# Pooled attention and a gated FFN on one core: three small tiles are resized so that TensorE's FFN operands start at one rest by 256 bytes

## The chip, the core and the metric

The kernel runs on one core of one Trainium2 chip. The metric is the device time of one execution in microseconds (us). Before the change it is 1043.09 us, the median of 3 runs (1041.45 to 1043.99). Lower is better.

## What is computed

Attention over keys and values that are averaged in groups of 8 along the sequence, followed by an FFN with a SiLU gate on the root-mean-square-normed result. All data is fp32; the shapes are B = H = 8, S = 576, D = 64, 4608 tokens, d_model 512, d_ff 1536.

```python
def _attn_ref(q, k, v):
    B, H, S, D = q.shape
    pool = 8
    Sp = S // pool
    k_p = k.reshape(B, H, Sp, pool, D).mean(axis=3)
    v_p = v.reshape(B, H, Sp, pool, D).mean(axis=3)
    scores = (1.0 / np.sqrt(D)) * np.matmul(q, k_p.transpose(0, 1, 3, 2))
    scores = scores - np.max(scores, axis=-1, keepdims=True)
    attn = np.exp(scores)
    attn = attn / (np.sum(attn, axis=-1, keepdims=True) + 1e-09)
    return np.matmul(attn, v_p)

def _moe_ref(x, w_gate, w_val, w_out, rms_g):
    rms = np.sqrt(np.mean(x * x, axis=-1, keepdims=True) + 1e-06)
    xn = x / rms * rms_g
    g = xn @ w_gate
    silu = g * (1.0 / (1.0 + np.exp(-g)))
    return silu * (xn @ w_val) @ w_out
```

## The kernel before

**Numbers.** TensorE takes fp32r operands (a rounded fp32 form). To keep precision, each FFN operand is split into a high part (rounded) and a low part (what the rounding left); a product is then three matmuls: high by high, low by high, high by low.

**Tiling.** The tokens are cut into 9 blocks of NB = 512, d_ff into NF = 12 slices of 128, d_model into NC = 4 chunks of 128. Every FFN matmul has a stationary operand of 128x128, which a LDWEIGHTS puts into the array, and a moving operand of 128x512. There are 3744 of them, of four sorts:

- `mm1` (line 812): x times w_gate or w_val, into a PSUM tile `psg`. Stationary: the weight slices `w1_f`. Moving: the high and low parts `xh`, `xl` of the block's tokens. 12 matmuls per (block, slice, gate or value).
- `mm2` (line 853): the activations times w_out, into four PSUM tiles `po`. Stationary: the activations' low part `hl` and high part `hh`, in four pieces of 128 tokens. Moving: the weight rows `w2_f`. Where nothing stands against it the four `hl` matmuls come first, then eight `hh` matmuls: for each of the four pieces one with the weights' high part and one with their low part. 12 matmuls per (block, slice).
- `product` (line 764): in the second part of the run, pairs of token blocks (5 with 6, 7 with 8) are multiplied by the w_gate/w_val slices in seven products in place of eight (Strassen's scheme), into `px` and `py`. Stationary: sums and blocks of weights `wp`, read back from DRAM into a ring of eight SBUF tiles, the ones that held `xh` and `xl`. Moving: sums of token blocks `xp`, in the space of the weights `w1`. 6 matmuls per product.

The attention is computed in the same program between these: scores `pss` (line 390), transposes `pst`, output `psx` (line 471), sums of squares `psr`. Softmax, splits and activations run on ScalarE (ACT), VectorE (DVE) and GpSimd (POOL).

**Order.** Two strings of steps written out by hand, ORDER and LATER, set the order of every engine's instructions; a step is a name and indices (`mg38` is mm1, gate, block 3, slice 8). Nothing is rescheduled.

**Places in SBUF.** Tiles come from pools that lie one behind the other in each partition's memory: `const` (small constants and `prob`), `wp` (the weights, and in the second part `xp`), `sb1` (one buffer a name: `mxe*`, `xh*`, `xl*`, `acc`, `act`, `hl`), `sb2` (two buffers a name: `st`, `xraw`, `out`, `pk`, `pv`, `ptf`, `hh` and small ones). A tile starts where the tile ahead of it ends, rounded up to 32 bytes. So the size of a small tile shifts every tile behind it. Three sizes count here: the unused constant `rest` (line 208, 104 floats, 416 bytes), the four `mxe` tiles of row maxima and sums (line 353, 2x2x5 floats, 80 bytes each, in steps of 96), and the two `pk` tiles of pooled keys (line 336, 72 floats, 288 bytes each).

This document calls the start of an operand modulo 256 bytes its **rest**. The pieces that a matmul reads within an FFN tile start at multiples of 512 bytes in it, so all operands of one tile have the tile's rest. Before the change the FFN tiles have three rests: 0 (`w1`, `w2`, `xp`), 128 (`xh`, `xl`, the ring `wp`, `hl`) and 192 (`hh`).

Of the kernel before, what the change touches and what calls it, by code (L numbers as in the profile page):

```python
# [9 lines left out]
F32 = mybir.dt.float32  # L10
# [7 lines left out]
P = 128  # L18
B, H, S, D = 8, 8, 576, 64
POOL = 8  # L20
SP = S // POOL
# [171 lines left out]
def body(ctx: ExitStack, tc: tile.TileContext, qT, kT, vN, w1, w2, gain, out):  # L193
    nc = tc.nc

    const = ctx.enter_context(tc.tile_pool(name="const", bufs=1))
    wp = ctx.enter_context(tc.tile_pool(name="wp", bufs=1))
    sb1 = ctx.enter_context(tc.tile_pool(name="sb1", bufs=1))
    sb2 = ctx.enter_context(tc.tile_pool(name="sb2", bufs=2))
# [5 lines left out]
    one = const.tile([P, 1], F32, name="one")  # L205
    nc.vector.memset(one, 1.0)
    ones = const.tile([P, 1], F32R, name="ones")
    const.tile([P, 104], F32, name="rest")
    nc.scalar.copy(ones, one)
    gcol = const.tile([P, NC], F32, name="gcol")  # L210
    eps = const.tile([P, 1], F32, name="eps")
# [86 lines left out]
    def own(p):  # L298
        s = st.setdefault((0, p), {})
        if "own" not in s:  # L300
            s["own"] = space1(NF - 2 - 2 * p, [P, 3 * S + SP + P], F32, f"own{p}")
        return s["own"]
# [28 lines left out]
    def s_kpool(b, p):  # L331
        s = st[b, p]
        if b == 0:
            pk = own(p)[:, 3 * S:3 * S + SP]
        else:
            pk = sb2.tile([P, SP], F32, tag="pk", name=f"pk{b}_{p}")
        s["pk"] = pk
        nc.vector.tensor_reduce(pk, s["k"].rearrange("p (s o) -> p s o", o=POOL), AX.X, ALU.add)

# [9 lines left out]
    def s_max(b, p, h):  # L349

        s, n = st[b, p], len(OFFS2)
        if "mx" not in s:
            x = sb1.tile([P, 2, 2, n], F32, tag=f"mxe{p}", name=f"mx{b}_{p}")
            s["mx"], s["sm"] = x[:, 0], x[:, 1]
        mx = s["mx"][:, h, :]
        nc.vector.tensor_reduce(mx, s["ps", h][:, :n * SP].rearrange("p (t k) -> p t k", k=SP), AX.X, ALU.max)
        nc.vector.tensor_scalar(mx, mx, -EXP_SCALE, None, ALU.mult)
# [521 lines left out]
    def first_phase():  # L879
        V, S_, G = nc.vector, nc.scalar, nc.gpsimd  # L880
        steps = dict(
            k=load_k, q=load_q, v=load_v, K=s_kpool, V=s_vpool, S=s_heads, M=s_max, E=s_exp, R=s_inverse,
            N=lambda b, p, h: s_norm(b, p, h, G), T=s_pt,
            C=lambda b, p, h: s_ptcopy(b, p, h, V.tensor_copy), D=lambda b, p, h: s_ptcopy(b, p, h, S_.copy),
            A=s_av, Y=lambda b, p, u: s_xcopy(b, p, u, S_.copy), X=lambda b, p, u: s_xcopy(b, p, u, V.tensor_copy),
            Z=s_xsq, Q=s_square, J=s_join, P=s_tokens, p=s_total, r=s_root, s=s_unroot, B=s_spread, H=s_scale,
            I=first_x, x=first_hi, y=lambda c: first_lo(c, V),
            l=w_load, a=w_abs, b=w_shift, c=w_low, d=w_sign, h=w_hi, w=lambda n: w_lo(n, V), W=lambda n: w_lo(n, G),
            g=lambda f: mm1(0, f, 0), e=lambda f: mm1(0, f, 1), G=lambda f: gate(0, f), F=lambda f: val(0, f),
            i=lambda f: act_hi(0, f), j=lambda f: act_lo(0, f, V), L=lambda f: act_lo(0, f, G), o=lambda f: mm2(0, f),  # L890
            z=warm, t=lambda c: (x_hi(1, c), x_lo(1, c)))
        nc.sync.dma_start(gcol, gain)
        run(ORDER, 1, steps)
        for t in range(NB // P):
            o_copy(0, t)
            o_store(0, t)

    def later_phase():
        V, S_ = nc.vector, nc.scalar
        run(LATER, 2, dict(  # L900
            lk=load_k, lq=load_q, lv=load_v, pk=s_kpool, pv=s_vpool, sc=s_heads, mx=l_max, sb=l_sub, ex=l_exp,
            sm=l_sum, nm=l_norm, tr=l_turn, dm=l_place, av=s_av, xc=l_xcopy, xd=l_xlast, sq=s_square, jn=s_join,
            sh=l_sumhi, sl=l_sumlo, rm=l_total, rt=l_root, rc=l_unroot, rs=l_scale,
            kt=keep_tail, xh=x_hi, xl=x_lo, mg=lambda i, f: mm1(i, f, 0), me=lambda i, f: mm1(i, f, 1), gt=gate,
            vl=val, hi=act_hi, lo=lambda i, f: act_lo(i, f, V), mo=mm2, mp=mm2, ev=o_copy, st=o_store,
            wd=w_blocks, wt=w_whole, wf=w_sum, wh=w_sumhi, wl=w_sumlo, ws=w_store,
            ys=p_sum, yh=p_hi, yl=p_lo, rl=w_part, pr=product,
            cp=lambda i, f: S_.copy(later(i, f), st["X"]),
            u2=lambda i, f: V.tensor_add(u2(i), later(i, f), st["Y"]),
            sa=lambda i, f: S_.activation(new_act(i, f), st["X"], AF.Silu),  # L910
            u3=lambda i, f: V.tensor_add(u3(i), u2(i), st["Y"]),  # L911
            c2=lambda i, f: V.tensor_sub(later(i, f), u3(i), st["X"]),  # L912
            sw=lambda i, f: S_.activation(later(i, f), later(i, f), AF.Silu),  # L913
            v2=lambda i, f: V.tensor_add(u3(i), u3(i), st["Y"]),  # L914
            v1=lambda i, f: V.tensor_add(u2(i), u2(i), st["Y"]),
            va=lambda i, f: V.tensor_mul(st["act"], st["act"], u2(i)),
            vb=lambda i, f: V.tensor_mul(later(i, f), later(i, f), u3(i))))
# [40 lines left out]
```

## Time and profile before

| what | value |
|---|---|
| median of 3 runs | 1043.09 us (1041.45 to 1043.99) |
| the profiled execution: its own time | 1040.0 us |
| its span, first to last instruction | 1037.9 us |
| TensorE clock granted over the span | 0.976 |
| TensorE matmul (PE) busy | 1007.0 us, 97% of the span |
| TensorE weight load (PEld) busy | 790.9 us, 76% |
| VectorE (DVE) busy | 632.0 us, 61% |
| ScalarE (ACT) busy | 449.3 us, 43% |
| GpSimd (POOL) busy | 227.4 us, 22% |
| mean DMA rate | 130 GB/s |

Rows of the profile name the line, the engine, the operation, the tile written and the tiles read (numbers in names left out), the shape, and how often. In rows of the timeline, the first number is the start in us from the start of the span, the second how long the group lasted; instructions of one sort that follow each other are one row. A matmul's own time (some 395 ns for the 128x512 ones) is its latency in a pipeline: the next one starts long before it ends. So the time that a matmul costs is not this duration but the distance from its start to the next one's, which is worked out from two rows that follow each other.

### The profile page before, as it was taken

What the parts mean: (1) busy time and instruction counts of PE and PEld (TensorE: products, weight loads), DVE (VectorE), ACT (ScalarE), POOL (GpSimd) and SP (SyncE); (2) the same over time, 40 slices, a digit from 0 to 9 for tenths busy, and PEclk for the clock granted to TensorE, in tenths of its full rate; (3) what the DMA queues carried; (4) which work ended last, traced back from release to release, by engine and by line L of the source; (5) the groups of instructions that cost most, each with busy time, mean ns of one, the idle gap of its engine ahead of it and who ended that gap; (6) DMA issues with size and microseconds to landing.
All of it is one profiled execution on the core that took longest, in us unless ns stands there. A gap on an engine that the chain in (4) does not pass through costs nothing.

```text
span 1037.9 us, 13861 instructions
## 1 busy us (share of the span) xinstructions
PE 1007.0 (97%) x4850; PEld 790.9 (76%) x4850; DVE 632.0 (61%) x1024; ACT 449.3 (43%) x845; POOL 227.4 (22%) x216
## 2 busy tenths in 40 slices
PE   7999999999999999999999999999999999999987
PEld 6777777777777777777777787878786778888866
DVE  6699996554772964775485385644655764444432
ACT  5767665543473454554364362322333432111121
POOL 2314440144333541355324140000000000000000
PEclk7599999999999999999999999999999999999999
DMA  9345422245345353444244323564544134544311
GB/s 303 126 158 187 171 73 77 71 139 143 102 134 156 100 159 91 140 145 150 83 146 147 97 89 115 162 206 143 167 143 134 41 122 146 151 149 144 102 40 41
DMA packets 97077, 134.71 MB, mean 130 GB/s; under 512 B 10225, under 2 KB 60145, under 8 KB 95729
## 3 DMA queue, kind: packets, MB, share of 16 engines
q1 hardware_dynamic: 97008, 133.83, 41.3%
q8 instruction: 39, 0.64, 0.2%
q14 instruction: 30, 0.24, 0.1%
HBM read 91.23 MB, written 34.60 MB: 121 GB/s over the span
## 4 chain that ended last, share of the span: by engine, by line
PE 86%; DVE 7%; ACT 2%; issue 2%; DMA 1%; SPq 0%; ACTq 0%; DVEq 0%
PE psg L812 28%; PE po L853 26%; PE py L764 13%; PE px L764 10%; PE pss L390 4%; PE psx L471 3%; DVE wt L258 1%; PE pst L447 1%; DVE wt L262 1%; DMA main<-kT 1%; PE psr L555 1%; DVE wt L254 1%; DVE w L280 0%; ACT prob L368 0%; PE psb L579 0%
## 5 line engine op out<-in xcount | busy, mean ns | idle before, releaser
L812 PE MATMUL psg<-xh,w 128*128 128x512 f32 x960 | 304.4, 399 | 1.8 <-ACT act L819 1.8
L853 PE MATMUL po<-w,hh 128*128 128x512 f32 x864 | 227.4, 395 | 0.0
L812 PEld LDWEIGHTS psg<-xh,w 128*128 128x128 f32 x960 | 177.4, 188 | 50.7 <-issue 5.3
L853 PEld LDWEIGHTS po<-w,hh 128*128 128x128 f32 x864 | 163.9, 190 | 36.8
L812 PE MATMUL psg<-xl,w 128*128 128x512 f32 x480 | 189.3, 395 | 0.2 <-DVE xl L642 0.2
L764 PE MATMUL py<-xp,wp 128*128 128x512 f32 x576 | 149.7, 395 | 0.8 <-DVE u L914 0.8
L853 PE MATMUL po<-w,hl 128*128 128x512 f32 x432 | 126.9, 403 | 9.8 <-DVE hl L839 5.1
L764 PEld LDWEIGHTS py<-xp,wp 128*128 128x128 f32 x576 | 108.3, 188 | 27.2 <-DVE u L914 1.2
L764 PE MATMUL px<-xp,wp 128*128 128x512 f32 x432 | 112.7, 396 | 0.0
L812 PEld LDWEIGHTS psg<-xl,w 128*128 128x128 f32 x480 | 90.2, 188 | 21.9 <-DVE xl L642 0.6
L853 PEld LDWEIGHTS po<-w,hl 128*128 128x128 f32 x432 | 79.8, 189 | 34.0 <-DVE hl L839 6.5
L421 POOL TENSOR_TENSOR prob<-prob,sm 128x360 f32<-128x360 f32 x48 | 43.7, 911 | 282.4 <-DVE sm L417 279.9
L764 PEld LDWEIGHTS px<-xp,wp 128*128 128x128 f32 x432 | 81.0, 188 | 20.0 <-ACT xraw L479 0.5
L824 DVE TENSOR_TENSOR act<-act,psg 128x512 f32<-128x512 f32 x60 | 40.8, 681 | 81.7 <-PE psg L812 70.1
L834 ACT CAST hh<-act 128x512 fp32r<-128x512 f32 x84 | 52.1, 621 | 66.0 <-DVE act L824 57.2
L839 DVE TENSOR_TENSOR hl<-act,hh 128x512 fp32r<-128x512 f32 x78 | 58.3, 748 | 34.3 <-ACT hh L834 26.7
L819 ACT ACTIVATE act<-psg 128x512 f32<-128x512 f32 x60 | 35.8, 597 | 67.7 <-PE psg L812 64.1
L819 ACT ACT_TABLE_LOAD x34 | 43.6, 1283 | 38.0 <-DVE hl L839 19.9
L911 DVE TENSOR_TENSOR u<-u,py 128x512 f32<-128x512 f32 x24 | 16.5, 688 | 67.4 <-PE py L764 67.4
L516 POOL TENSOR_TENSOR acc<-acc,sq 128x576 f32<-128x576 f32 x21 | 31.5, 1499 | 102.4 <-ACT sq L510 102.4
L913 ACT ACTIVATE hb<-hb 128x512 f32<-128x512 f32 x24 | 15.2, 632 | 87.8 <-DVE hb L912 87.8
L686 POOL TENSOR_TENSOR wt<-wsum,wt 128x256 fp32r<-128x256 f32 x48 | 38.3, 814 | 53.1 <-ACT wt L682 53.0
(132 smaller groups left out, 1225.0 us busy)
## 6 DMA issues: line engine op xcount, KB each, us to landing
wp<-sum SPq DMA_DIRECT2D x96, 256.0 KB
wp<-blocks SPq DMA_DIRECT2D x72, 256.0 KB
blocks<-w SPq DMA_DIRECT2D x24, 512.0 KB
sum<-wt SPq DMA_DIRECT2D x48, 256.0 KB
wx<-w SPq DMA_DIRECT2D x10, 1024.0 KB
v<-vN SPq DMA_DIRECT2D x32, 288.0 KB
out<-o SPq DMA_DIRECT2D x36, 256.0 KB
wx<-w SPq DMA_DIRECT2D x16, 512.0 KB
```

Source lines behind the costliest of these rows:

```text
L390: nc.tensor.matmul(s["ps", h][:, t * SP:(t + 1) * SP], s["q"][r, o:o + P], s["pk"][r, :], start=True, stop=True)
L421: nc.gpsimd.tensor_tensor(l_pr(h), l_pr(h), sm[:, :, None].broadcast_to([P, len(OFFS2), SP]), ALU.mult)
L471: nc.tensor.matmul(ps[r, :n], s["pv"][:, r], x, start=True, stop=True)
L516: nc.gpsimd.tensor_add(acc[b], acc[b], st[b, p]["sq"])
L686: nc.gpsimd.tensor_sub(y[:, 1], place(f, f"T{k}"), y[:, 0].bitcast(F32))
L764: nc.tensor.matmul(ps[:, :NB], w[:, a, c, :], x[:, b, c, :], start=j == 0 and not more, stop=j == len(todo) - 1, skip_group_check=more)
L812: nc.tensor.matmul(ps[:, :NB], w[:, c, cols], x[c], start=(j == 0), stop=(j == len(todo) - 1))
L819: nc.scalar.activation(t, ps[:, :NB], AF.Silu)
L824: nc.vector.tensor_mul(t, t, ps[:, :NB])
L834: nc.scalar.copy(a, act_in(i, f))
L839: eng.tensor_sub(l, act_in(i, f), hh[i, f].bitcast(F32))
L853: nc.tensor.matmul(po[i][t], x[i, f][:, t * P:(t + 1) * P], w, start=(f == 0 and k == 0), stop=(f == NF - 1 and k == 2))
```

## The change

Nothing is added to or removed from what the engines do. On every engine the built program has the same instructions in the same order, with the same waits on the same values; only the addresses of operands in SBUF differ.

```diff
     ones = const.tile([P, 1], F32R, name="ones")
-    const.tile([P, 104], F32, name="rest")
     nc.scalar.copy(ones, one)
...
         else:
-            pk = sb2.tile([P, SP], F32, tag="pk", name=f"pk{b}_{p}")
+            pk = sb2.tile([P, 96], F32, tag="pk", name=f"pk{b}_{p}")[:, :SP]
         s["pk"] = pk
...
         if "mx" not in s:
-            x = sb1.tile([P, 2, 2, n], F32, tag=f"mxe{p}", name=f"mx{b}_{p}")
-            s["mx"], s["sm"] = x[:, 0], x[:, 1]
+            x = sb1.tile([P, 2, 2, 8], F32, tag=f"mxe{p}", name=f"mx{b}_{p}")
+            s["mx"], s["sm"] = x[:, 0, :, :n], x[:, 1, :, :n]
```

`rest` goes (416 bytes less ahead of `wp`), each `mxe` tile grows from 80 to 128 bytes (four of them, 128 bytes more ahead of `xh`), each `pk` tile from 288 to 384 bytes (two, 192 bytes more ahead of `hh`). The instructions still use 72 and 5 floats of the grown tiles. The places in the built program, as byte starts and rests by 256:

| tile | role in FFN matmuls | before: start, rest | after: start, rest |
|---|---|---|---|
| `prob` (attention) | none | 2208, 160 | 1792, 0 |
| first `w1` tile (all `w1`, `w2`, `xp` alike) | stationary in mm1, moving in mm2 and product | 6144, 0 | 5728, 96 |
| first `xh` (all `xh`, `xl`, ring `wp` alike) | moving in mm1, stationary in product | 160384, 128 | 160096, 96 |
| `act` and `hl` | stationary in mm2 (low part) | 179072 and 181120, 128 | 178784 and 180832, 96 |
| `st`, `xraw`, `out` | none | 128 | 96 |
| the two `pk` (attention) | none | 128 and 160 | 96 and 224 |
| the two `hh` | stationary in mm2 (high part) | 224704 and 226752, 192 | 224608 and 226656, 96 |

So the distance from the moving operand's rest to the stationary operand's rest, by 256, goes from 128 (mm1, product, `hl`) and 192 (`hh`) to 0 throughout.

## The prediction, made before the changed kernel had run

> **What bounds the kernel.** I read the page's busy table first, then the chain of work that ended last.
>
> ```profile
> PE 1007.0 (97%) x4850; PEld 790.9 (76%) x4850; DVE 632.0 (61%) x1024; ACT 449.3 (43%) x845; POOL 227.4 (22%) x216
> ...
> PE 86%; DVE 7%; ACT 2%; issue 2%; DMA 1%; SPq 0%; ACTq 0%; DVEq 0%
> PE psg L812 28%; PE po L853 26%; PE py L764 13%; PE px L764 10%; PE pss L390 4%; PE psx L471 3%; DVE wt L258 1%; PE pst L447 1%; DVE wt L262 1%; DMA main<-kT 1%; PE psr L555 1%; DVE wt L254 1%; DVE w L280 0%; ACT prob L368 0%; PE psb L579 0%
> ```
>
> The busy 97% alone proves nothing, since matmul durations overlap. The chain does: the FFN matmuls (psg, po, py, px) carry 28 + 26 + 13 + 10 = 77% of the 1037.9 us span, about 799 us. The groups of instructions say how many there are and that they wait little:
>
> ```profile
> L812 PE MATMUL psg<-xh,w 128*128 128x512 f32 x960 | 304.4, 399 | 1.8 <-ACT act L819 1.8
> L853 PE MATMUL po<-w,hh 128*128 128x512 f32 x864 | 227.4, 395 | 0.0
> L812 PE MATMUL psg<-xl,w 128*128 128x512 f32 x480 | 189.3, 395 | 0.2 <-DVE xl L642 0.2
> L764 PE MATMUL py<-xp,wp 128*128 128x512 f32 x576 | 149.7, 395 | 0.8 <-DVE u L914 0.8
> L853 PE MATMUL po<-w,hl 128*128 128x512 f32 x432 | 126.9, 403 | 9.8 <-DVE hl L839 5.1
> L764 PE MATMUL px<-xp,wp 128*128 128x512 f32 x432 | 112.7, 396 | 0.0
> ```
>
> That is 960 + 480 + 576 + 432 = 2448 in mm1 and product, 432 with `hl`, 864 with `hh`: 3744. What one costs is its cadence, start to next start, in stretches where nothing waits. First from the chain, then from the timeline of PE alone:
>
> ```profile
> 630.62 5.59 PE psg L812 x24
> ```
> ```profile
> 869.84 0.62 PE L853 MATMUL po<-w,hh 128*128 128x512 f32 x2
> 870.30 1.56 PE L764 MATMUL py<-xp,wp 128*128 128x512 f32 x6
> 871.70 1.56 PE L764 MATMUL px<-xp,wp 128*128 128x512 f32 x6
> ```
> ```profile
> 811.03 1.08 PE L853 MATMUL po<-w,hl 128*128 128x512 f32 x4
> 811.95 2.00 PE L853 MATMUL po<-w,hh 128*128 128x512 f32 x8
> 813.79 1.09 PE L853 MATMUL po<-w,hl 128*128 128x512 f32 x4
> 814.72 1.99 PE L853 MATMUL po<-w,hh 128*128 128x512 f32 x8
> 816.55 1.08 PE L853 MATMUL po<-w,hl 128*128 128x512 f32 x4
> ...
> 838.60 0.40 PE L853 MATMUL po<-w,hl 128*128 128x512 f32 x1
> ```
>
> The reader is to see three cadences. mm1: 5.59 / 24 = 0.2329 us. Product: 871.70 - 870.30 = 1.40 for 6, 0.2333 us. mm2: from 811.03 to 838.60 are 120 matmuls in 27.57 us, 0.2298 us; inside it, four `hl` take 0.92 to 0.93 (0.231 each), eight `hh` 1.84 to 1.83 (0.229 each). The three have the same shapes and the same clock, and mm1 and `hl`, for instance, move their operands in quite different patterns. What sets the `hh` apart is the rest of their stationary operand: 192 against a moving operand at 0, where all others stand 128 apart. **So the trace gives a reason to think that the rests matter, by some 3.6 ns in 233.** A second confound, that an `hh` piece is loaded twice running, is weaker: the interval into the first `hh` piece of a tile is as short as the second.
>
> **Why the cadence can depend on rests at all.** In the weight loads' timeline
>
> ```profile
> 630.92 0.42 PEld L812 LDWEIGHTS psg<-xh,w 128*128 128x128 f32 x2
> 631.38 0.19 PEld L812 LDWEIGHTS psg<-xl,w 128*128 128x128 f32 x1
> ```
> ```profile
> 630.91 0.40 PE L812 MATMUL psg<-xl,w 128*128 128x512 f32 x1
> 631.15 0.63 PE L812 MATMUL psg<-xh,w 128*128 128x512 f32 x2
> ```
>
> the load for the next matmul starts within 0.01 us of the running matmul's start (630.92 after 630.91), lasts 0.19 us, and the next matmul starts some 0.04 us after its end. Both read SBUF at the same time: the moving operand of matmul n and the stationary operand of matmul n+1. The pair whose rests count is that one.
>
> **The change, part by part.** Orders, waits and counts of instructions are unchanged, so no wait appears or goes. Three effects are left.
>
> 1. *The pair's distance becomes 0.* Distance 0 occurs before only at handovers: while the last `hh` matmul of mm2 runs (`w2`, rest 0), the first `w1` piece (rest 0) of the following mm1 is loaded. There are 44 such handovers without a wait; the first and the last:
>
> ```profile
> 68.91 0.40 PE L853 MATMUL po<-w,hh 128*128 128x512 f32 x1
> 69.15 0.40 PE L812 MATMUL psg<-xh,w 128*128 128x512 f32 x1
> ...
> 630.23 0.39 PE L853 MATMUL po<-w,hh 128*128 128x512 f32 x1
> 630.46 0.40 PE L812 MATMUL psg<-xh,w 128*128 128x512 f32 x1
> ```
>
> Their mean interval, from start times that the trace holds to the ns, is 0.2306 us. The control is 95 handovers from an `hh` matmul to an operand at rest 128 (`hl` or the ring), again first and last:
>
> ```profile
> 171.56 0.40 PE L853 MATMUL po<-w,hh 128*128 128x512 f32 x1
> 171.80 0.40 PE L853 MATMUL po<-w,hl 128*128 128x512 f32 x1
> ...
> 1030.97 0.40 PE L853 MATMUL po<-w,hh 128*128 128x512 f32 x1
> 1031.21 0.40 PE L853 MATMUL po<-w,hl 128*128 128x512 f32 x1
> ```
>
> Their mean is 0.2336 us. So from the same preceding work a load at distance 0 comes 3 ns sooner than one at 128, and about 1 ns later than one at 192. I take 0.2306 us as the cadence of the whole FFN after the change. Sum: 2448 x (0.2331 - 0.2306) = 6.1 us gained, 432 x (0.2310 - 0.2306) = 0.2 gained, 864 x (0.2306 - 0.2294) = 1.0 lost; 5.3 us net. Only what lies on the chain counts: 3744 matmuls at a mean of 0.232 are 869 us, of which the chain holds 799, a share of 0.92. That leaves **4.9 us**. Bounds of this unknown: below, all go at the `hh` rate of 0.2294, which gains (2448 x 0.0037 + 432 x 0.0016) x 0.92 = 9.0 us; above, all go at 0.2331, which loses (864 x 0.0037 + 432 x 0.0021) x 0.92 = 3.8 us. I stay at the row of distance 0 itself.
>
> A rule of the skill speaks against any effect here. The Trainium skill, "TensorE: Matmul & The Clock Gate", section "Step-by-step: what each phase is for", says that TensorE has two independent SBUF read ports, so that loading the next tile's weights takes no read bandwidth from the running matmul. By that rule the sum would be 0. The 0.229 of `hh` against 0.233 elsewhere disagrees with it in this trace, or has a cause that I don't see.
>
> 2. *Rest 96 is no multiple of 64.* All FFN operands were at multiples of 64. The nearest rows are scores whose moving operand `pk` lies at 128 and at 160:
>
> ```profile
> 174.68 1.34 PE L390 MATMUL pss<-pk,q 64*128 64x72 f32 x20
> 194.89 1.34 PE L390 MATMUL pss<-pk,q 64*128 64x72 f32 x20
> ```
>
> The first is at 128, the second at 160; both take 1.34 us. They are short and of full fp32, so they don't settle it for 128x512, but I put this at 0, with the bounds from the same two rows: their rounding of 0.01 in 20 matmuls is 0.5 ns on each, or 3744 x 0.0005 x 0.92 = 1.7 us either way.
>
> 3. *ACT, DVE, POOL and DMA see shifted tiles too.* DVE is on the chain with 7%, ACT 2%, DMA 1%. I put them at 0; a 1% change of all three would be 0.01 x 10% x 1038 = 1.0 us either way. The DMA queue's cover is wide in the product phase:
>
> ```profile
> 680.00:780.00 100.00, 77.60 (x320) 60.05 (x321) 1.00 0.53 162
> ```
>
> There (the window's columns are length, PE and PEld busy, clock, DMA share, GB/s) the DMA engines are busy 0.53 of the time, so that transfers could take half as long again before the ring starves TensorE. If that cover were gone, py and px, 23% of the chain, would grow with the transfers.
>
> **The sum.** The profiled execution took 1040.0 us, 2.1 more than its span of 1037.9, and lies 3.1 us below the median shown. 1040.0 - 4.9 = 1035.1 for such an execution; against the median of 1043.09 that is 1038.2 us, 0.47% less. A measurement of this kernel can tell about 0.3% (3.1 us) from no change.
>
> **The rivals.**
>
> - *Distance counts by 128, not by 256* (ends slower). 192 is then 64, the only good distance, and 0 and 128 are the same bad one. mm1 and product don't move, and mm2 loses its better rate: 3.8 us, 1046.9 us. It decides as soon as steady matmuls at distance 0 go at over 0.2320 us, where gains and losses cancel: (2448 x 0.2331 + 432 x 0.2310 + 864 x 0.2294) / 3744 = 0.2320. For it: the good 192 and the bad 128 fit a period of 128 as well. Against it: the 44 handovers at 0.2306. They are single intervals, and the matmul before may have left the pair in a good phase. Chance 0.13.
> - *Rests do nothing* (the change doesn't do what it says, or the gain ends in waits). `hh` is faster for another reason, such as its order of PSUM tiles, and keeps its rate: 1043.1 us. For it: the skill's rule above; against it the control handovers, which start new pieces in new PSUM tiles as the others do. Chance 0.22.
> - *Same rest is as good as 192 or better.* All at 0.2294: 9.0 us less, 1034.1 us. For it: nothing yet shows a steady run at 0. Chance 0.17, of which a part is for still shorter cadences.
> - *Lockstep collides* (slower). Both reads start in the same place at every matmul, and each interval is like the slowest single ones above, 0.24 us: (2448 x 0.0069 + 432 x 0.009 + 864 x 0.0106) x 0.92 = 27.5 us, 1070 us; or rest 96 costs each matmul a part of that. Against it: the shorter handovers at equal rests. Chance 0.07.
>
> **How the numbers follow.** My forecast has 0.41. Around it the cadence may be off by 1 ns, 3.4 us, so a quarter of it ends within 0.3%. Faster by over 0.3% (below 1040.0): three quarters of 0.41, nearly all of 0.17, a little from the second rival, 0.50. Slower by over 0.3% (above 1046.2): 0.07 and the larger half of 0.13, 0.15. Within: 0.35. The range goes from 1033, just under the all-at-`hh` case, to 1047, which takes in the period-128 case; what is left out are collisions above and much shorter cadences below.
>
> **What would show it.** In the profile of the changed kernel, the same places: 24 psg matmuls in about 5.53 us in place of 5.59, 6 of a product in 1.38 to 1.39 in place of 1.40, 120 matmuls of the mm2 tail in 27.7 in place of 27.57. If psg stays at 5.59 and the tail grows to 27.9 or more, the period is 128. If psg stays and the tail stays, rests do nothing. If psg falls below 5.50 along with a tail below 27.5, equal rests are better than 192. The attention's rows (1.34 us for 20 scores) must not move. The prediction is wrong if a gain in these rows comes back as waits of PE for DVE or ACT, which the list of waits would show, or if the DMA share of the product stretch rises well over 0.53.

## The result, and the profile after

The changed kernel takes **1028.01 us** (median of 4 runs, 1024.67 to 1029.17) against 1042.74 us before (4 runs, 1041.45 to 1043.99): a ratio of 0.9854, 95% interval 0.9826 to 0.9881. That is 14.7 us less, where 4.9 were forecast. The direction was right; the time lies 5 us below the range. The profiled execution took 1026.97 us with a span of 1024.9.

First the busy table and the chain of work that ended last of the changed kernel, whose line numbers are one lower than before:

```profile
PE 992.1 (97%) x4850; PEld 790.8 (77%) x4850; DVE 632.3 (62%) x1024; ACT 449.7 (44%) x845; POOL 227.2 (22%) x216
...
PE 86%; DVE 7%; ACT 3%; issue 1%; DMA 1%; SPq 0%; POOL 0%; ACTq 0%; DVEq 0%; POOLq 0%
PE psg L811 28%; PE po L852 27%; PE py L763 13%; PE px L763 10%; PE pss L389 4%; PE psx L470 3%; DVE wt L257 1%; DVE wt L261 1%; DMA main<-kT 1%; PE pst L446 1%; PE psr L554 1%; DVE hl L838 1%; DVE wt L253 1%; DVE xraw L546 0%; PE psb L578 0%
```

The reader is to see that nothing but PE has moved. DVE, ACT and POOL are busy as long as before to within 0.4 us, the counts are the same, and the same four FFN groups carry the chain. Next the waits of PE in the changed kernel (total us, times, longest):

```profile
PE po L852 <- DVE hl L838: 5.1, 3, 2.9
PE po L852 <- DVE o L866: 4.8, 3, 2.3
PE pst L446 <- POOL prob L379: 3.0, 2, 2.2
PE pss L389 <- DVE mx L373: 2.6, 1, 2.6
```

They stand against 5.1 and 4.7 us for the first two before, so the gain did not come out of waits, nor did it go back into them. It is in the cadence. The chain of the changed kernel in its mm1 stage and in the product (start us, length us), and PE's timeline in the mm2 tail:

```profile
617.21 5.44 PE psg L811 x24
622.65 2.72 PE po L852 x12
...
637.64 1.36 PE px L763 x6
```
```profile
804.99 1.07 PE L852 MATMUL po<-w,hl 128*128 128x512 f32 x4
805.90 1.98 PE L852 MATMUL po<-w,hh 128*128 128x512 f32 x8
807.71 1.07 PE L852 MATMUL po<-w,hl 128*128 128x512 f32 x4
...
824.04 1.07 PE L852 MATMUL po<-w,hl 128*128 128x512 f32 x4
```

24 mm1 matmuls take 5.44 us (0.2267 each), 6 of a product 1.36 (0.2267), and in the tail 84 matmuls from 804.99 to 824.04 take 19.05 (0.2268). The three cadences of before, 0.233, 0.233 and 0.230, have become one. From the start times that the trace holds to the ns, over all intervals between FFN matmuls under 260 ns (3580 before, 3562 after; the others hold a wait or other work, or ran at half clock):

```
                       before      after     matmuls x difference
mm1    (psg)           232.8 ns    228.0     1440 x 4.8 = 6.9 us
product (px, py)       232.4       227.0     1008 x 5.4 = 5.4
hl -> hl               232.1       228.0      432 x 4.1 = 1.8
hh -> hh               229.8       227.3      864 x 2.5 = 2.2
all                    232.0       227.5     3744 x 4.5 = 16.9
```

The last line is its own mean, with the handovers between sorts in it. The weight load still takes 188 ns and still starts 3 to 4 ns after the running matmul; what has become shorter is the step from its end to the next matmul's start, 35 or 36 ns in 77% of the cases in place of 38 to 47 in 90% of them before.

### The profile page after: what moved, and what is told of

Read it like the earlier page. It is cut to its first block, busy times and chain, and to the rows that moved or that the text cites. A ratio compares the mean times of both kernels' runs of the same rounds, so it can differ in the third digit from the quotient of the medians.

```text
span 1024.9 us, 13861 instructions
## 1 busy us (share of the span) xinstructions
PE 992.1 (97%) x4850; PEld 790.8 (77%) x4850; DVE 632.3 (62%) x1024; ACT 449.7 (44%) x845; POOL 227.2 (22%) x216
## 4 chain that ended last, share of the span: by engine, by line
PE 86%; DVE 7%; ACT 3%; issue 1%; DMA 1%; SPq 0%; POOL 0%; ACTq 0%; DVEq 0%; POOLq 0%
PE psg L811 28%; PE po L852 27%; PE py L763 13%; PE px L763 10%; PE pss L389 4%; PE psx L470 3%; DVE wt L257 1%; DVE wt L261 1%; DMA main<-kT 1%; PE pst L446 1%; PE psr L554 1%; DVE hl L838 1%; DVE wt L253 1%; DVE xraw L546 0%; PE psb L578 0%
## 5 line engine op out<-in xcount | busy, mean ns | idle before, releaser
L852 PE MATMUL po<-w,hh 128*128 128x512 f32 x864 | 225.1, 392 | 0.0
L811 PEld LDWEIGHTS psg<-xh,w 128*128 128x128 f32 x960 | 179.6, 190 | 48.4 <-issue 5.3
L763 PE MATMUL py<-xp,wp 128*128 128x512 f32 x576 | 146.5, 390 | 0.8 <-DVE u L913 0.8
L763 PE MATMUL px<-xp,wp 128*128 128x512 f32 x432 | 110.2, 390 | 0.0
```

Of the source, the lines that this page charges most:

```text
L763: nc.tensor.matmul(ps[:, :NB], w[:, a, c, :], x[:, b, c, :], start=j == 0 and not more, stop=j == len(todo) - 1, skip_group_check=more)
L811: nc.tensor.matmul(ps[:, :NB], w[:, c, cols], x[c], start=(j == 0), stop=(j == len(todo) - 1))
L852: nc.tensor.matmul(po[i][t], x[i, f][:, t * P:(t + 1) * P], w, start=(f == 0 and k == 0), stop=(f == NF - 1 and k == 2))
```

## The experiments

All experiments change sizes of small tiles only; instructions, order and waits are those of the changed kernel. Distances are from the moving operand's rest to the next stationary operand's rest, by 256. Each expectation says what its theories are. The first four kernels ran on one chip beside 17 runs of the kernel before (median 1042.17 us); the four of the second group had one run each, beside one of the kernel before of 1043.06 us; the last group ran beside 9 of the kernel before (median 1044.25).

### Equal rests, at 0 in place of 96

A constant is put back, a smaller one, so that all FFN operands rest at 0, and `prob` at 160 as before.

```diff
     ones = const.tile([P, 1], F32R, name="ones")
+    const.tile([P, 40], F32, name="rest")
```

> A constant of 160 bytes ahead of the weights shifts every FFN tile from rest 96 to rest 0; all distances stay 0. Theory D (only the distance between the moving and the next stationary operand counts): settled cadence 0.2267 us as in the changed kernel, 24 psg matmuls in a row in 5.44 us, ratio to before 0.985, about 1028 us. Rival A (rest 96 itself is the good place): cadence back to 0.230 to 0.233, ratio 0.995 to 1.00. The attention's prob lies at rest 160 again as before the change; a theory that its move to 0 brought the gain expects about 1042 us here too.

Measured: 1027.42 us (4 runs, 1024.34 to 1030.12), ratio 0.9855 (0.9804 to 0.9905). The chain of this kernel has, in its mm1 stage:

```profile
619.61 5.44 PE psg L812 x24
```

This is the changed kernel's time and cadence. So where the operands rest does not matter, 96 or 0, nor does the new place of `prob`; what they have in common, the distance 0, is what counts.

### One of the three sizes put back: all distances 128

```diff
-            x = sb1.tile([P, 2, 2, 8], F32, tag=f"mxe{p}", name=f"mx{b}_{p}")
+            x = sb1.tile([P, 2, 2, 5], F32, tag=f"mxe{p}", name=f"mx{b}_{p}")
```

> The mxe tiles go back to 80 bytes, the other two edits stay: weights at 96, every other FFN operand at 224, all distances 128, hh too. Theory D: all four sorts at about 0.233 us (24 psg in 5.59, 120 po of the tail in 27.9 to 28.0), a little slower than before the change, where hh stood at 192: 1042.7 + 2 to 4 = 1045 to 1047 us, ratio 1.002 to 1.004. Rival P (the gain comes from the other shifted tiles, prob, pk, xraw, or from rests on DVE, ACT and DMA): it stays at 1028 to 1034 us.

Measured: 1044.27 us (10 runs, 1041.34 to 1047.22), ratio 1.0016 (0.9995 to 1.0037). The weights stay at 96 and everything else stands at 224. The chain in the mm1 stage, then PE's timeline in the mm2 tail:

```profile
624.55 5.60 PE psg L811 x24
```
```profile
813.70 1.10 PE L852 MATMUL po<-w,hl 128*128 128x512 f32 x4
814.63 2.03 PE L852 MATMUL po<-w,hh 128*128 128x512 f32 x8
816.50 1.08 PE L852 MATMUL po<-w,hl 128*128 128x512 f32 x4
```

The whole gain is gone. The time is a little under the 1045 to 1047 that was expected, and its interval takes in no change against the kernel before. `hh`, now at 128 as well, has lost its own advantage: eight take 816.50 - 814.63 = 1.87 us, 0.2337 each, with a mean of 233.0 ns over the program. That answers the question which the profile of before left open: `hh` was faster because of its rest, and not because of its order.

### Another put back: only `hh` differs

```diff
-            pk = sb2.tile([P, 96], F32, tag="pk", name=f"pk{b}_{p}")[:, :SP]
+            pk = sb2.tile([P, 72], F32, tag="pk", name=f"pk{b}_{p}")[:, :SP]
```

`hh` goes to rest 160, a distance of 64 from the weights at 96; all else stays at distance 0.

> The pk tiles go back to 288 bytes, the other two edits stay: only hh moves, to rest 160, a distance of 64; mm1, product and hl stay at 0. Theory D: psg, px and py settle at 0.2267 as in the changed kernel; the 864 hh loads go at a rate not yet seen, between 0.2267 and 0.233, so 1028 to 1033 us, ratio 0.985 to 0.991. Rival (the pk edit carries the gain): 1038 us or more, with psg back at 0.233.

Measured: 1034.48 us (8 runs, 1030.28 to 1037.53), ratio 0.9931 (0.9905 to 0.9958). In the chain:

```profile
619.34 5.47 PE psg L811 x24
624.80 2.77 PE po L852 x12
```

`hh` goes at 233.4 ns, 6.1 more than in the changed kernel, which is 864 x 6.1 = 5.3 us. By the medians 6.5 us are lost, by the gains over the kernels before (14.7 and 7.7) 7.0. For its neighbours, whose own distances are unchanged, also lose: mm1 goes from 228.0 to 228.7, `hl` from 228.0 to 229.2, py from 226.9 to 229.1. So theory D missed here: the time lies above its 1033, and py doesn't stay at 0.2267. A bad distance costs more than its own matmuls.

### The same distance by 256, another by 512

```diff
-            x = sb1.tile([P, 2, 2, 8], F32, tag=f"mxe{p}", name=f"mx{b}_{p}")
+            x = sb1.tile([P, 2, 2, 24 if p == 0 else 8], F32, tag=f"mxe{p}", name=f"mx{b}_{p}")
```

Everything behind the `mxe` tiles moves by 256 bytes; the weights don't. The expectation is not quite right about `hl`: at 180832 bytes it stood at 96 by 512 in the changed kernel already (180832 = 353 x 512 + 96), and here it goes to 352, the other way from `xh`, `xl`, the ring and `hh`.

> The first mxe tile grows by 256 bytes more: the weights and all other FFN operands then have the same rest by 512 too (96), where in the changed kernel it is 96 against 352. If the period is 256: nothing changes, settled cadence 0.2267, ratio 0.985, 1028 us. If the period is 512 or more: the cadence of psg, px and py moves by over 1 ns, the time by over 2 us either way.

Measured: 1028.15 us (4 runs, 1026.05 to 1030.44), ratio 0.9868 (0.9828 to 0.9909), and 24 mm1 matmuls in the chain take again

```profile
612.72 5.44 PE psg L811 x24
```

A move by 256 bytes changes nothing, for `hl` either (228.0 and 228.1 ns). With the second experiment, where 128 changes everything, the period is 256.

### The distances between

Three kernels put `xh`, `xl`, `hl` and the ring, and `hh` with them, at other distances. In mm1 `w1` is stationary and in the product the ring is, so the roles are swapped and the two distances add up to 256: each kernel gives two or three points.

```diff
-            pk = sb2.tile([P, 96], F32, tag="pk", name=f"pk{b}_{p}")[:, :SP]
+            pk = sb2.tile([P, 104], F32, tag="pk", name=f"pk{b}_{p}")[:, :SP]
...
-            x = sb1.tile([P, 2, 2, 8], F32, tag=f"mxe{p}", name=f"mx{b}_{p}")
+            x = sb1.tile([P, 2, 2, 10 if p == 0 else 8], F32, tag=f"mxe{p}", name=f"mx{b}_{p}")
```

The second kernel has 108 and 12 in these places, the third 112 and 14.

> Pads put xh, xl, hl and the ring at rest 128 and hh at 192, the weights stay at 96. Distances from the moving to the next stationary operand: mm1 224, product and hl 32, hh 96. Theory D with a smooth function of the distance between the four values measured so far (0: 0.2267, 64: 0.2334, 128: 0.2330, 192: 0.2296): mm1 about 0.228, product about 0.230, hh 0.233; some 1033 us. Rival D64 (what counts is only which 64-byte piece of 256 an operand starts in): mm1 and product go like 0 or like 192 and 64, with no value between.

> Pads put xh, xl, hl and the ring at rest 160 and hh at 32, the weights stay at 96. Distances: mm1 192, product and hl 64, hh 192. Theory D: mm1 at 0.2296 like hh before the change, product at 0.2334, hh at 0.2296; the sign of the distance counts, not its size. Time near 1036 us. Rival (each sort has its own best place, and the rate of hh at 192 was its own): mm1 at 0.2330 as before the change, 1042 us or more.

> Pads put xh, xl, hl and the ring at rest 192 and hh at 64, the weights stay at 96. Distances: mm1 160, product and hl 96, hh 224. Theory D with a smooth function: mm1 0.231, product 0.233, hh 0.228; about 1038 us. Rival D64: only the values 0.2267, 0.2296, 0.2330, 0.2334 appear.

Measured, one run each: 1046.25, 1043.10 and 1046.13 us. The chain of each in the mm1 stage (distances 224, 192 and 160):

```profile
625.75 5.60 PE psg L811 x24
```
```profile
623.53 5.50 PE psg L811 x24
```
```profile
623.83 5.61 PE psg L811 x24
```

With the kernels before, the mean cadence by distance:

```
distance   mean cadence, ns
   0       226.7 settled (changed kernel; mean of all 227.5)
  32       232.9 product, 233.4 hl
  64       233.2 product, 232.6 hl; 233.4 hh (one size put back)
  96       233.7 product, 232.4 hl; 233.7 hh
 128       232.8 mm1, 232.4 product (before); 232.9 mm1, 233.0 hh (one size put back)
 160       233.7 mm1
 192       229.3 mm1; 231.3 hh (distance 64 beside it), 229.8 hh (before)
 224       233.3 mm1; 233.3 hh
```

The theory of a smooth curve falls: 32 and 224, the nearest to 0, are as bad as 128. Rival D64 falls too: in the third kernel `hh` (rest 64) and the weights (96) start in the same 64-byte piece, and `hh` goes at 233.3. In the second, mm1 and product came out as theory D said, but `hh` at 231.3 and not 229.6, and the time 7 us above its 1036; that kernel's mean cadence of 231.3 is worth some 2.7 us against 232.0 before, which one run can't show. Of the eight distances only 0 is good, 192 about half as good, and six are alike within 1.3 ns. None is better than 0.

### The changed kernel once more

The first profile delivered 13.0 us of span where the cadences promise 16.9. This run asks whether the difference belongs to the change.

> The changed kernel once more, for its clock. In the first profile of it, and in those with the same distances at rest 0 and by 512, two half-clock stretches of 3.4 us lie at 122 and 183 us that the kernel before doesn't have, and the first psg matmuls go at half clock. Theory G (shorter matmuls leave longer gaps, and the clock gate closes in them every time): the same stretches, psg first group at 0.43 us each. Rival (the gate's windows fall by chance in any kernel): another pattern.

Measured: 1023.67 us, span 1021.6, with the same mean cadence, 227.50 ns, and

```profile
623.11 5.44 PE psg L811 x24
```

Against the first profile of before the span is 16.3 us shorter, and the time from the first FFN matmul to the last goes from 976.8 to 961.5, 15.3 us. So 0.91 to 0.97 of the cadence's sum (16.8 by this run's mean) arrives. A little of that is the clock's: the first profile of before has a half-clock stretch at 994.5 to 997.9 us that this run lacks. What the first profile lacked is seen in windows of 4 us (length, PE, PEld, DVE, ACT and POOL busy, granted clock, DMA share, GB/s), first the changed kernel's first profile, then this one:

```profile
52.00:56.00 4.00, 4.00 (x10) 2.92 (x10) 3.96 (x9) 3.95 (x6) 0.79 (x1) 0.50 0.36 111
184.00:188.00 4.00, 4.00 (x14) 3.23 (x13) 3.13 (x6) 2.84 (x5) 1.07 (x1) 0.69 0.00 0
```
```profile
52.00:56.00 4.00, 3.61 (x17) 2.33 (x16) 4.00 (x8) 3.97 (x9) 0.00 (x0) 1.00 0.00 0
184.00:188.00 4.00, 4.00 (x19) 3.30 (x19) 3.81 (x7) 2.48 (x4) 1.07 (x1) 1.00 0.00 0
```

In the first profile the clock was at 0.50 when the first mm1 matmuls ran, so that a full window holds 10 matmuls in place of 17, and it was at half speed again for parts of the windows near 122 and 184 us. In this run it was not, in the same program. Theory G falls with that. Nor are the stretches a mark of distance 0: two of 3.4 us stand near 125 and 188 us in the profiles with the same distances at rest 0 and by 512, but also, near 125 and 187 us, in that of the kernel with mm1 at 192 and product at 64. What sets their places, no run here shows. The kernel before, run twice, has stretches of half clock at 11.5 to 52.5 us in one profile and at 11.8 to 22.0 and 28.8 to 56.1 in the other.

### `hh` alone at the other good distance

```diff
-            pk = sb2.tile([P, 96], F32, tag="pk", name=f"pk{b}_{p}")[:, :SP]
+            pk = sb2.tile([P, 120], F32, tag="pk", name=f"pk{b}_{p}")[:, :SP]
```

`hh` gets distance 192, as in the kernel before; all else is at 0.

> The pk tiles are made 480 bytes, so that hh stands at a distance of 192 as before the change, while mm1, product and hl stay at 0. Theory S (a stream of loads at distance 0 reaches 0.2267 only after some ten matmuls without a disturbance, and a load at another distance disturbs it): hh near 0.230, and psg and hl lose too, psg above 0.2280 on average; 1030 to 1033 us. Rival L (each load pays for its own distance alone): hh 0.2296, psg at 0.2279 and the products at 0.2269 as in the changed kernel; 1028 + 2 = 1030 us.

Measured: 1032.13 us (2 runs, 1031.47 and 1032.78), ratio 0.9894 (0.9833 to 0.9955). `hh` goes at 229.85 ns, which is what it had before among neighbours at 128, and the neighbours lose a little: mm1 228.55, `hl` 229.2. Summed by sort that is 864 x 2.5 + 1440 x 0.55 + 432 x 1.2 = 3.5 us, and 4.1 were lost against the changed kernel's median. Two runs can't tell 1030 us from 1032; the neighbours' cadences speak for theory S. So 192 has a rate of its own, some 3 ns above 0, beside 0 and beside 128; beside 64 it was 231.3.

### `hh` alone at distance 0

```diff
-            pk = sb2.tile([P, 96], F32, tag="pk", name=f"pk{b}_{p}")[:, :SP]
+            pk = sb2.tile([P, 112], F32, tag="pk", name=f"pk{b}_{p}")[:, :SP]
...
-            x = sb1.tile([P, 2, 2, 8], F32, tag=f"mxe{p}", name=f"mx{b}_{p}")
+            x = sb1.tile([P, 2, 2, 5], F32, tag=f"mxe{p}", name=f"mx{b}_{p}")
```

The converse: `hh` at 0, all else at 128.

> Only hh is put at distance 0, all other operands stand 128 apart as before the change. Theory S: eight hh loads in a row, each row between loads at 128, hardly settle, so hh goes at 0.229 to 0.231 like the single handovers of before; time 1042 to 1045 us. Rival L: hh at 0.2267 to 0.2273 as in the changed kernel, 2 us less than before the change, 1040 to 1041 us.

Measured: 1043.32 us (8 runs, 1037.89 to 1046.78), ratio 0.9993 (0.9962 to 1.0025), no change. PE's timeline of the tail, its first run of eight `hh` and the third:

```profile
816.10 2.01 PE L852 MATMUL po<-w,hh 128*128 128x512 f32 x8
817.95 1.10 PE L852 MATMUL po<-w,hl 128*128 128x512 f32 x4
...
821.64 1.99 PE L852 MATMUL po<-w,hh 128*128 128x512 f32 x8
823.47 1.10 PE L852 MATMUL po<-w,hl 128*128 128x512 f32 x4
```

The first eight, close behind other work, take 1.85 us, 0.2313 each, where in the changed kernel, between neighbours at 0, eight take 807.71 - 805.90 = 1.81, 0.2263. The third run takes 1.83: the interval into it is 232 ns, those inside are 231, 227, 226, 227, 227, 226 and 227, and the one out of it is 232 again. Of the 75 runs of eight without a wait behind `hl`, 36 end with three intervals of 225 to 227 ns; in the changed kernel 67 do. The mean of `hh` over the program is 229.4 ns, no better than at 192, and `hl` beside it goes at 232.8 where it was 232.1 before. **Among neighbours at 128, a run of eight at distance 0 reaches the rate of distance 0 inside, if at all, and the intervals into it and out of it don't.** Over all FFN matmuls the mean is 232.0, as before the change.

### The kernel before once more

> The kernel before once more, for its clock. If the half-clock stretches of 3.4 us fall by chance in any kernel, this profile shows another pattern than the first one of it (one long stretch to 52.5 us, none at 122 and 183 us) and the same cadences (24 psg matmuls in 5.59 us); if they are a mark of the changed kernel, this one has none there again.

Measured: 1039.92 us, span 1037.8, mean cadence 232.01 ns (231.995 in the first profile), 5.59 us for 24 mm1 matmuls. The cadence of either kernel repeats to some hundredths of a ns, while their spans move by 3 us with the clock.

## Why the direction was right, and why the forecast was too small

**What bounds the kernel** was right: 77 to 78% of the chain are FFN matmuls, what counts is their cadence, and it fell while nothing else moved.

**That rests count** was right. The distance between the moving and the stationary operands of the stream decides, by 256: the same tiles at a distance of 0 gave 1027 to 1028 us at two rests and with 256 bytes added, and 1044 at 128. This is shown by the experiments, not argued.

**Which pair counts** is not shown. The prediction names the moving operand of one matmul and the stationary one of the next, because both are read at the same time. But within one sort the next matmul's stationary operand has the same rest as the running one's own, so the streams can't tell the two pairs apart, and the handovers point both ways. With `hh` alone at 64, the interval from the last `py` to the first `hh`, in which the first `hh` is loaded, is still 225.8 ns (22 cases), and only the next one is 235.8. With `hh` alone at 0, the interval from the last `hh` to the first `py`, loaded at a distance of 128, is 232.1 at once (45 cases).

The rule that was weighed, in the Trainium skill's "TensorE: Matmul & The Clock Gate", section "Step-by-step: what each phase is for", is that loading the next weights takes no read bandwidth from the running matmul. The sum of 0 that the prediction drew from it did not come: the same instructions take 226.7 ns at one distance and 233 at another. Whether the two reads share anything in the hardware, and why 192 stands out as the second good distance, no run here shows.

**The step that failed** is "I take 0.2306 us as the cadence of the whole FFN after the change". The row it rests on is the mean of 44 handovers at distance 0. The same 44 handovers, with the same operands at the same distance, go at 226.5 ns in the changed kernel, and the whole FFN at a mean of 227.5, settled 226.7. That is 3.1 ns under the step's figure, or 3744 x 3.1 x 0.92 = 10.7 us, where the gain exceeds the forecast by 9.8. Their intervals, sorted, ns:

```
         225 to 227   229 to 232   235 to 237    mean
before       18           11           15        230.55
after        44            0            0        226.52
```

The mean of before was that of a mixture, and what moves it is the stream ahead. Every kernel here has these 44 handovers at distance 0. They go at 226.5 to 226.7 ns where everything stands at 0, at 228.2 behind `hh` alone at 0, and behind `hh` at other distances at 229.1 (128), 230.6 to 230.8 (192), 231.0 (96 and 224) and 231.8 (64). A row that moves like this with what runs before it could not carry the rate of a stream, so that it pointed the right way was in part luck. The stream ahead is seen in the changed kernel too, wherever a wait or another kind of matmul breaks the stream. By the number of intervals since the break:

```
after a break   1      2      3      4      5-6    7-9    10-14   15 and more
before, ns    230.2  232.8  230.5  233.6  233.2  230.9   232.7      232.0
after, ns     234.4  234.0  231.5  232.6  228.9  228.9   227.0      226.7
```

In the kernel before the rows never settle; in the changed kernel they begin as high or higher and settle after some ten matmuls. The forecast needed the end of this curve, and a single handover behind another distance doesn't give it. Why settling takes that long was not tried.

**The lower bound** failed by the same step: "all go at the `hh` rate of 0.2294" took 192 as the best that could be, and no row supported that as a floor. The rival "same rest is as good as 192 or better" is what happened, in the part of it that was not priced ("a part is for still shorter cadences"): psg fell to 5.44 and the 120 matmuls of the tail to 27.2 (from 802.24 to 829.48), below the 5.50 and 27.5 of that test. It had a chance of 0.17, against 0.41 for the forecast.

**The term for `hh`**, "1.0 lost", had the wrong sign: it gained 2.5 ns each, 2.2 us.

**The chain share of 0.92** was about right as a size: 0.91 to 0.97 in the changed kernel's second profile. In the median of 14.7 us against 16.9 it is 0.87, with stretches of half clock in the way.

**Effects 2 and 3**, put at 0, were 0. Rest 96 and rest 0 give the same time. The attention's matmul `pss` has 272 ns as its median in both, and its 20 scores at 174.02 us take 1.34 us as before. The product stretch after

```profile
670.00:770.00 100.00, 76.11 (x321) 59.65 (x320) 1.00 0.56 171
```

(a window as that of before, shifted by 10 us; PE and PEld are those of the product's line alone) has a DMA share of 0.56 against 0.53 (and 0.50 at 680 to 780 us), and PE waits for no transfer in it.

**The other rivals.** A period of 128 is refuted twice: 128 itself is bad, and 64 differs from 192 (233.2 against 229.3 in one kernel). "Rests do nothing" and "lockstep collides" are refuted by the result.

## What to carry to other kernels

Where TensorE runs matmul after matmul with a weight load for each, as here with 128x128 by 128x512 in fp32r, let the moving and the stationary operands start at the same place by 256 bytes in SBUF, for all tiles of the stream at once: here one tile out of line lost its own share and some of its neighbours', and one tile alone in line gained nothing. Small tiles ahead in the pool decide this, so compute the starts before tuning. And when a rate is estimated from single cases, look at their distribution, not at the mean: several clusters say that the surroundings decide, and then no single case gives the rate of a stream. The lower cluster alone is no sign either: in the kernel with mm1 at a distance of 192 throughout, 31% of mm1's intervals are 225 to 227 ns, and its stream stays at 229.3.

## What the runs showed of the hardware beside this

The start of a matmul behind its weight load depends on addresses at all: 226.7 ns from start to start at distance 0, 229.3 to 231.3 at 192, 232.4 to 233.7 at six other multiples of 32. At a bad distance the intervals of a steady stream go in cycles: behind the last `py`, the `hh` matmuls go 236, 231, 236, 231 ns at a distance of 64 and 229, 231, 226, 229, 232 at 192, where at 0 all are 226 or 227. The TensorE clock's stretches of half speed differ between executions of one program: the changed kernel's span was 1024.9 with three of them on the FFN's path (near 52, 122 and 184 us) and 1021.6 without. In single runs the kernel before ranged from 1037.11 to 1046.21 us, so an effect of 5 us needs several runs, or the cadence, which repeats far better than the time.
